# Attention and two feed-forward layers on one core: where the first feed-forward block's operand is made

## The chip, the cores and the metric

The kernel runs on one core of one Trainium2 chip. A core has a matmul engine (TensorE, PE in the rows), three engines for element-wise work (VectorE or DVE, ScalarE or ACT, GpSimd or POOL), a queue engine that here issues all transfers (SyncE, SP), 16 DMA engines, an on-chip memory (SBUF) and eight accumulator banks (PSUM) of 128 partitions by 512 floats. DRAM lies outside. The metric is the device time of one launch in microseconds; the time before is the median of three runs.

## The reference

Inputs are q, k, v of shape 4 x 8 x 576 x 64 (batches, heads, tokens, width), a memory per head, and the weights of two feed-forward layers (512 to 2048 to 512). Cut to what matters:

```python
a = softmax(q @ k.T / 8, causal); local = a @ v
mem = (phi(q) @ M_prev) / (phi(q) @ z_prev + 1e-6)        # phi(x) = elu(x) + 1
x = g * mem + (1 - g) * local                             # g = sigmoid(beta), per head
x = x as 2304 tokens x 512
x = (s * relu(x @ w_in)**2 + b) @ w_out                   # layer 1
h = x @ w_in2; x = (max(h, 0) + alpha * min(h, 0)) @ w_out2   # layer 2
```

All is float32 in and out.

## The kernel before, in words

**Precision.** The feed-forward matmuls work on the type fp32r, in which a float32 operand is given as two parts: a rounded one (h) and what the rounding left (l). A product is three matmuls: h by h, h by l, l by h. Weights and activations are split like this: a cast on ScalarE (or VectorE) writes h, a subtract on VectorE writes l.

**Attention.** Batches 0 to 3 are worked on in order, in each four pairs p of heads. A pair's 576 tokens are cut into two sets g (256 tokens, and 320 tokens with the last 64 in a chunk of their own). For each set TensorE makes scores, VectorE adds the mask and finds the extreme, ScalarE takes the exponential, the weights are scaled and turned, and TensorE accumulates the output of both heads (128 rows by 256 or 320 tokens) in a PSUM bank called `ok` (L697 to L722). In batch 0 any of the eight banks may be used, in later batches three. For batches 0 and 1 (`WHOLE`) the bank is copied as it is into an SBUF slot `xt` by ScalarE or VectorE, whichever is free first (L728 to L731). Once both sets are there, the pair's 576 tokens are stored into the DRAM tensor `x1` (L754).

**Feed-forward.** Layer 1 works on blocks of tokens: block 0 has 512 (of batch 0's 576), blocks 1 and 2 have 320, the others 288. Layer 2 has blocks of 512. `load_x` (L919 to L954) fetches a block's operand from `x1`: for block 0 these are four loads of 128 rows by 512 tokens (L934), each followed by a cast on ScalarE (L943) and a subtract on VectorE (L945) into the tile `xr`. A load waits for the stores that it reads. For each f of 16, g1 makes the hidden values (12 matmuls, L844 to L846, into one bank `hb`), Relu and Square on ScalarE (L858, L859) and a split (L866, L867) follow, and g2 accumulates the output in four banks (12 matmuls, L878 to L880).

**Weights.** Layer 1's weights come in 32 halves (16 f, w_in and w_out), as pairs of integers, and are put together and split: five operations each, four on VectorE and a cast on ScalarE (L790 to L804); the last, L802, completes the half. The load of f waits until pair min(3, f) of batch 0 is in `x1` (L786).

**Order.** Nothing runs by program order: every operation is entered with an engine, a duration, what it reads and writes, and a priority (`op`, L90), and a planner (`order`, L122) simulates the engines and writes a fixed list for each. An operation's default priority is its number, so attention comes in order; block splits have priority -3, the hidden values' -1, the block matmuls 10,000,000 and up, so that they fill the time that attention leaves on TensorE. Batch 0's slots may lie in memory that the last weights use later (`early`). A slot is taken and freed in the plan. The keys `("xh", s, d)` and `("xl", s, d)` stand for the operand's parts; block 0's g1 waits for those of s = 0 and 1 and all four d (L848 to L851), since its operand takes the room of two smaller blocks.

Of the kernel before, what the change touches and what calls it, by code (L numbers as in the profile page):

```python
# [6 lines left out]
F32 = mybir.dt.float32  # L7
# [5 lines left out]
ALU = mybir.AluOpType  # L13
AX = mybir.AxisListType

B, H, S, D = 4, 8, 576, 64
# [5 lines left out]
NBIG, NB = 512, 320  # L22
# [19 lines left out]
WHOLE = (0, 1)  # L42
# [29 lines left out]
class Plan:  # L72
# [17 lines left out]
    def op(self, eng, dur, fn, r=(), w=(), prio=None, bytes_=0, claim=()):  # L90
        i = len(self.ops)
        deps, late = set(), set()
        for k in r:
            if k in self.writer:
                deps.add(self.writer[k])
            self.readers.setdefault(k, []).append(i)
        for k in w:
            if k in self.writer:
                deps.add(self.writer[k])
            late.update(self.readers.get(k, ()))  # L100
            self.writer[k] = i
            self.readers[k] = []
        late -= deps
        late.discard(i)
        deps.discard(i)
        slots = []
        for k in list(r) + list(w):
            s = k[0] if isinstance(k, tuple) else k
            if isinstance(s, Slot) and s not in slots:
                slots.append(s)  # L110
                s.left += 1
        self.ops.append((eng, dur, fn, deps | late, i + self.lean if prio is None else prio, bytes_, slots, late, claim))
        return i
# [181 lines left out]
def t_dve(n, rate=1.04, extra=0.0):  # L295
    return 69 + n * rate + extra


def t_act(n, fixed=93.0, extra=0.0):
    return fixed + n * 0.834 + extra  # L300


def build(tc, kp, vd, qp, mzd, beta8, sb2, win1, wout1, win2, wout2, alpha, outT):
    nc = tc.nc
    win1, wout1, win2, wout2 = (w.bitcast(I32) for w in (win1, wout1, win2, wout2))
    V, A, T = nc.vector, nc.scalar, nc.tensor
    plan = Plan(NSLOT, 3 * XF)
    plan.edge = NSLOT - XS
    op = plan.op
    ATT, MOE, LATE = 0, 10 ** 7, 400  # L310

    with tc.tile_pool(name="sb", bufs=1) as sb, tc.tile_pool(
        name="ps", bufs=1, space=bass.MemoryType.PSUM
    ) as ps, tc.tile_pool(name="dr", bufs=1, space=bass.MemoryType.DRAM) as dr, tc.manual_schedule():
        x1 = dr.tile([128, NP, NT], F32, name="x1")
# [53 lines left out]
        def at(s, n, dt=F32):  # L369

            if s.place < NSLOT:
                t, j = (pool, s.place) if s.place < NSLOT - XS else (poolx, s.place - NSLOT + XS)
                v = t[:, j * GW:(j + s.size) * GW]
            else:
                f, j = divmod(s.place - NSLOT, 3)
                v = room[KF - XF + f][:, j * GW:(j + s.size) * GW]
            return (v if dt == F32 else v.bitcast(dt))[:, 0:n]
# [8 lines left out]
            out=mask[:, S - 128:], in_=mask[:, S - 128:], pattern=[[-1, 128]],  # L386
# [3 lines left out]
        for r in (0, 64):  # L390
            op("POOL", 150, lambda r=r: nc.gpsimd.tensor_copy(out=mask2[r:r + 64, S // 2 - 64:], in_=mask[r:r + 64, S - 128 + r:S - 64 + r]),
               r=["mask"], w=["mask2"])
# [7 lines left out]
        def consts2():  # L400
# [9 lines left out]
            out=ident, in_=ident, pattern=[[-1, 128]], compare_op=ALU.is_equal, fill=0.0, base=0, channel_multiplier=1),  # L410
           r=["ident"], w=["ident"])
# [8 lines left out]
        def bank_at(bk):  # L420
            return banks[bk.place - NSLOT - 3 * XF]
# [6 lines left out]
        def either(kind, a_dur, a_fn, d_dur, d_fn, **kw):  # L428

            ways = {"ACT": (a_dur, a_fn)}  # L430
            if kind in FLEX:
                ways["DVE"] = (d_dur, d_fn)
            plan.either(ways, **kw)
# [180 lines left out]
        def pair(b, p, sqp, sa, sv, xt):  # L614
# [4 lines left out]
               r=gate(b * H + 2 * p, KG, KG0), prio=-8 if b + p == 0 else None, w=[sk], bytes_=512 * S)  # L619
# [5 lines left out]
            for g, cs in enumerate(SETS):  # L625
                ch0 = cnt["ch"]
                o0 = AT[cs[0]]
# [97 lines left out]
                    return at(xt, S)[:, o0:o0 + qn]  # L725


                if b in WHOLE:  # L728
                    either("x", t_act(qn, 50), lambda xr=xr, qn=qn, ok=ok: A.copy(out=xr(), in_=bank_at(ok)[:, 0:qn]),
                           t_dve(qn), lambda xr=xr, qn=qn, ok=ok: V.tensor_copy(out=xr(), in_=bank_at(ok)[:, 0:qn]),  # L730
                           r=[ok], w=[(xt, g)])  # L731
                else:
                    un = vsc[:, j, 1:2]
                    either("x", t_act(qn, 50, 93), lambda xr=xr, qn=qn, ok=ok: A.activation(
                        out=xr(), in_=bank_at(ok)[:, 0:qn], func=AF.Copy, scale=un),
                        t_dve(qn, 1.04, 60), lambda xr=xr, qn=qn, ok=ok: V.tensor_scalar(
                        out=xr(), in0=bank_at(ok)[:, 0:qn], scalar1=un, scalar2=None, op0=ALU.mult),
                        r=[ok, ("un", j)], w=[(xt, g)])
# [3 lines left out]
        def attention(b):  # L742
            marks.append(len(plan.ops))
            memory(b)
            for p in range(NP):

                plan.lean = VLEAN
                sv = values(b, p)
                plan.lean = FLEAN
                sp_, sa = features(b, p)  # L750
                plan.lean = 0
                xt = Slot(RES["xt"], b == 0)
                pair(b, p, sp_, sa, sv, xt)
                op("SP", 475, lambda p=p, xt=xt: nc.sync.dma_start(out=x1[:, p, b * S:(b + 1) * S], in_=at(xt, S)),  # L754
                   r=[(xt, g) for g in range(2)], w=[("x1", b, p)], bytes_=512 * S)

# [54 lines left out]
        def x_of(n, xs, lo, d):  # L813

            if xs == 2:
                return cut(xr2(), n, KD * lo + d)
            if n == NBIG:
                return cut(xr_, n, KD * lo + d)
            return cut(xr_, n, 2 * KD * xs + KD * lo + d, NB)
# [99 lines left out]
        def load_x(layer, blk, t0, n, xs):  # L919
            step = GW // n  # L920
            for u in range(0, KD, step):
                s = Slot(RES["x"])
                if layer == 1:
                    src = x1[:, u:u + step, t0:t0 + n]
                    rk = [("x1", b, u + e) for e in range(step) for b in range(t0 // S, (t0 + n - 1) // S + 1)]
                else:
                    src = y1[:, u:u + step, t0:t0 + n]
                    rk = [("y1", j, u + e) for e in range(step) for j, (a, m) in enumerate(BLOCKS[1])
                          if a < t0 + n and t0 < a + m] + ["claimed"]

                def xr(s=s):
                    return at(s, step * n).rearrange("p (d n) -> p d n", d=step)

                op("SP", 475, lambda xr=xr, src=src: nc.sync.dma_start(out=xr(), in_=src), r=rk,  # L934
                   w=[s] + [("xset", x) for x in ((0, 1, 3) if xs == 3 else (xs,))], bytes_=512 * step * n,
                   prio=-2 if layer == 2 and blk > 0 else None)
                for e in range(step):
                    d = u + e
                    def X(lo, d=d):
                        return x_of(n, xs, lo, d)  # L940

                    if layer == 1:
                        op("ACT", t_act(n), lambda X=X, e=e, xr=xr: A.copy(out=X(0), in_=xr()[:, e, :]),  # L943
                           r=[s], w=[("xh", xs, d)], prio=-3)
                        op("DVE", t_dve(n), lambda X=X, e=e, xr=xr: V.tensor_tensor(  # L945
                            out=X(1), in0=xr()[:, e, :], in1=X(0).bitcast(F32), op=ALU.subtract),
                           r=[s, ("xh", xs, d)], w=[("xl", xs, d)], prio=-3)
                    else:
                        bc = bcs[:, d:d + 1]
                        op("ACT", t_act(n, 93, 180), lambda X=X, e=e, xr=xr, bc=bc: A.activation(  # L950
                            out=X(0), in_=xr()[:, e, :], func=AF.Identity, bias=bc), r=[s, ("bcs", d)], w=[("xh", xs, d)], prio=-3)
                        op("DVE", t_dve(n, 1.04, 60), lambda X=X, e=e, xr=xr, bc=bc: V.scalar_tensor_tensor(
                            out=X(1), in0=xr()[:, e, :], scalar=bc, in1=X(0).bitcast(F32), op0=ALU.add, op1=ALU.subtract),
                           r=[s, ("xh", xs, d), ("bcs", d)], w=[("xl", xs, d)], prio=-3)  # L954

        def moe(layer, blk, xs):
            t0, n = BLOCKS[layer][blk]
            load_x(layer, blk, t0, n, xs)
            for f in range(KF):
                if layer == 1 and blk == 0:  # L960
                    weights(win1, wout1, f, 1)
                if f == 0 and (layer, blk) == (1, 1):
                    flush()
                    op("ACT", 400, ones, r=["one", ("g2", KF - 1)],
                       w=["gr"] + [(x, j) for x in ("gt", "gh", "gl") for j in range(2)])

                if layer == 1 and n == NBIG and pend[0] is not None:
                    flush()
                gj = g1(layer, n, xs, f)
                if pend[0] is not None:  # L970
                    flush()
                pend[0] = (layer, blk, f, gj)
# [78 lines left out]
```

## Time and profile before

| what | value |
|---|---|
| median of three runs | 1017.6 us (1016.55 to 1017.99) |
| the profiled execution's own time | 1017.4 us |
| its span, first to last instruction | 1015.7 us |
| mean granted TensorE clock | 0.993 of 2.4 GHz |
| TensorE busy | 997.8 us (98%), 6648 matmuls |
| VectorE busy | 584.1 us (58%) |
| ScalarE busy | 461.3 us (45%) |

The busy time of an engine is the time in which at least one of its instructions runs. Matmuls overlap: each row's duration is longer than the step to the next. Digits in the page's slices are tenths; one of forty slices is 25.4 us. The clock is given as a part of 2.4 GHz, so that 0.50 is 1.2 GHz.

### The profile page before, as it was taken

How to read it: one execution, taken by the hardware profiler on the slowest of the kernel's cores; microseconds unless marked ns; L12 is line 12 of the kernel's file. 1: busy time of each engine (PE TensorE's matmuls, PEld its weight loads, DVE VectorE, ACT ScalarE, POOL GpSimd, SP SyncE). 2: the span in 40 equal slices, each digit the busy share in tenths (PEclk: the TensorE clock that was granted, in tenths of full speed). 3: DMA queues.
4: the chain of work that ended last, by engine and by line, in shares of the span. 5: the costliest groups of instructions: out<-in, count | busy, mean ns of one | idle time of the engine just before them, and what ended most of it. 6: DMA issues, size and time to landing. Idle time of an engine off the chain costs nothing.

```text
span 1015.7 us, 16933 instructions
## 1 busy us (share of the span) xinstructions
PE 997.8 (98%) x6648; PEld 846.0 (83%) x6648; DVE 584.1 (58%) x1389; ACT 461.3 (45%) x1113; POOL 5.1 (0%) x29
## 2 busy tenths in 40 slices
PE   7979999999999999999999999999999999999998
PEld 5757777778889888899999998888888888888898
DVE  7999987566555556543121779965434533443454
ACT  7866766677666677644444653222101111210111
POOL 1000000000000000000000000000000000000000
PEclk9979999999999999999999999999999999999999
DMA  4475433163564436542000555312000200100010
GB/s 146 164 257 174 159 137 128 49 143 90 113 147 115 71 82 150 104 140 88 1 24 2 169 169 166 116 62 83 1 1 1 73 1 1 42 1 1 1 43 21
DMA packets 85599, 87.12 MB, mean 86 GB/s; under 512 B 56336, under 2 KB 63504, under 8 KB 85520
## 3 DMA queue, kind: packets, MB, share of 16 engines
q1 hardware_dynamic: 85520, 86.05, 29.3%
q8 instruction: 52, 0.85, 0.3%
q14 instruction: 27, 0.22, 0.1%
HBM read 58.76 MB, written 14.16 MB: 72 GB/s over the span
## 4 chain that ended last, share of the span: by engine, by line
PE 95%; DVE 3%; ACT 1%; DMA 0%; issue 0%; SPq 0%; ACTq 0%; DVEq 0%
PE yb L878 14%; PE yb L880 13%; PE yb L879 13%; PE hb L844 9%; PE hb L845 8%; PE hb L846 8%; PE sp L846 3%; PE sp L845 3%; PE sp L844 3%; PE sp L716 2%; PE sp L663 2%; PE ob L845 2%; PE ob L844 2%; PE ob L846 2%; PE ob L663 1%; PE sp L551 1%
## 5 line engine op out<-in xcount | busy, mean ns | idle before, releaser
L878 PE MATMUL yb<-gr,wt 128*128 128x512 f32 (+4 forms) x768 | 264.6, 345 | 0.1
L880 PE MATMUL yb<-gr,wt 128*128 128x512 f32 (+4 forms) x768 | 259.6, 338 | 0.0
L879 PE MATMUL yb<-gr,wt 128*128 128x512 f32 (+4 forms) x768 | 259.4, 338 | 0.0
L844 PE MATMUL hb<-xr,wt 128*128 128x288 f32 (+3 forms) x528 | 176.4, 334 | 1.4 <-ACT gt L858 1.4
L845 PE MATMUL hb<-xr,wt 128*128 128x288 f32 (+3 forms) x528 | 170.5, 323 | 0.0
L846 PE MATMUL hb<-xr,wt 128*128 128x288 f32 (+3 forms) x528 | 170.2, 322 | 0.0
L878 PEld LDWEIGHTS yb<-gr,wt 128*128 128x128 f32 x768 | 144.4, 188 | 23.8 <-issue 8.1
L867 DVE TENSOR_TENSOR gr<-gt,gr 128x288 fp32r<-128x288 f32 (+3 forms) x152 | 81.5, 536 | 140.0 <-ACT gr L866 139.4
L880 PEld LDWEIGHTS yb<-gr,wt 128*128 128x128 f32 x768 | 144.5, 188 | 14.7 <-DVE gr L867 0.2
L879 PEld LDWEIGHTS yb<-gr,wt 128*128 128x128 f32 x768 | 144.6, 188 | 13.4
L866 ACT CAST gr<-gt 128x288 fp32r<-128x288 f32 (+3 forms) x152 | 75.3, 495 | 144.8 <-DVE gt L864 136.1
L844 PEld LDWEIGHTS hb<-xr,wt 128*128 128x128 f32 x528 | 99.5, 188 | 17.2 <-issue 8.9
L846 PEld LDWEIGHTS hb<-xr,wt 128*128 128x128 f32 x528 | 99.6, 189 | 5.8
L858 ACT ACTIVATE gt<-hb 128x288 f32<-128x288 f32 (+2 forms) x112 | 49.8, 444 | 118.7 <-PE hb L846 118.0
L845 PEld LDWEIGHTS hb<-xr,wt 128*128 128x128 f32 x528 | 99.6, 189 | 4.3
L866 ACT CAST gr<-mz 128x512 fp32r<-128x512 f32 (+1 forms) x40 | 23.1, 578 | 158.0 <-DVE mz L864 157.9
L846 PE MATMUL sp<-xr,wt 128*128 128x512 f32 (+1 forms) x160 | 59.4, 371 | 0.0
L845 PE MATMUL sp<-xr,wt 128*128 128x512 f32 (+1 forms) x160 | 59.3, 371 | 0.0
L844 PE MATMUL sp<-xr,wt 128*128 128x512 f32 (+1 forms) x160 | 59.2, 370 | 0.0
L648 DVE CUSTOM_DVE_ANT_0 sp<-sp,mask 128x384 f32<-128x384 f32 (+4 forms) x81 | 40.8, 514 | 25.4 <-PE sp L663 14.8
L859 ACT ACTIVATE gt<-gt 128x288 f32<-128x288 f32 (+2 forms) x112 | 53.5, 478 | 2.4
L867 DVE TENSOR_TENSOR gr<-mz,gr 128x512 fp32r<-128x512 f32 (+1 forms) x40 | 25.6, 639 | 25.3 <-ACT gr L866 25.3
(352 smaller groups left out, 1452.7 us busy)
## 6 DMA issues: line engine op xcount, KB each, us to landing
pool<-wout SPq DMA_DIRECT2D x20, 512.0 KB, 4.5
pool<-win SPq DMA_DIRECT2D x19, 512.0 KB, 3.7
room<-wout SPq DMA_DIRECT2D x12, 512.0 KB, 4.1
room<-win SPq DMA_DIRECT2D x11, 512.0 KB, 3.8
pool<-y SPq DMA_DIRECT2D x18, 256.0 KB, 3.3
out_t<-pool SPq DMA_DIRECT2D x16, 256.0 KB, 2.1
x<-poolx SPq DMA_DIRECT2D x10, 288.0 KB, 2.5
pool<-qp SPq DMA_DIRECT2D x9, 288.0 KB, 4.2
```

The source lines that it names most:

```text
L648: op("DVE", t_dve(kn, 1.04, 60 if before is not None else 0), lambda: V.tensor_tensor_reduce(out=bank_at(bk)[:, 0:kn], in0=bank_at(bk)[:, ...
L663: T.matmul(bank_at(bks[odd])[:, 0:nk], half(sqp, odd, AT[c], 128), half(sk, odd, 0, nk), start=True, stop=True)
L844: T.matmul(H_, W_h, X_h, start=(d == 0), stop=False)
L845: T.matmul(H_, W_h, X_l, start=False, stop=False)
L846: T.matmul(H_, W_l, X_h, start=False, stop=(d == KD - 1))
L858: op("ACT", t_act(n, 50), lambda: A.activation(out=t_, in_=H_, func=AF.Relu), r=[hk, "gr"], w=[tk], prio=-1)
L859: op("ACT", t_act(n), lambda: A.activation(out=t_, in_=t_, func=AF.Square), w=[tk], prio=-1)
L866: op("ACT", t_act(n), lambda: A.copy(out=G_h, in_=t_), r=[tk], w=[("gh", gj)], prio=-1)
L867: op("DVE", t_dve(n), lambda: V.tensor_tensor(out=G_l, in0=t_, in1=G_h.bitcast(F32), op=ALU.subtract), r=[tk, ("gh", gj)], w=[("gl", gj)], ...
L878: T.matmul(Y, W_h, G_h, start=(f == 0), stop=False)
L879: T.matmul(Y, W_l, G_h, start=False, stop=False)
L880: T.matmul(Y, W_h, G_l, start=False, stop=(f == KF - 1))
```

## The change

For batch 0 the output bank `ok` is no longer copied as a whole. Of each set, the tokens that belong to block 0 (256 of the first set, 256 of the second) are cast from PSUM into the h part of `xr` by ScalarE, and VectorE subtracts that from PSUM into the l part. The 64 tokens left of the second set are copied to the slot `xt` by either engine and stored into `x1`; the store has 64 tokens in place of 576. `load_x` is not called for block 0 of layer 1. The two splits of a pair use the keys s = g = 0 and 1, and have the default priority in place of -3. All else is as it was, and the planner makes the whole order anew.

```diff
-                if b in WHOLE:
+                if b == 0:
+                    m = min(qn, NBIG - o0)
+
+                    def X(lo, o0=o0, m=m):
+                        return x_of(NBIG, 0, lo, p)[:, o0:o0 + m]
+
+                    op("ACT", t_act(m, 50), lambda X=X, m=m, ok=ok: A.copy(out=X(0), in_=bank_at(ok)[:, 0:m]),
+                       r=[ok], w=[("xh", g, p)])
+                    op("DVE", t_dve(m), lambda X=X, m=m, ok=ok: V.tensor_tensor(
+                        out=X(1), in0=bank_at(ok)[:, 0:m], in1=X(0).bitcast(F32), op=ALU.subtract),
+                       r=[ok, ("xh", g, p)], w=[("xl", g, p)])
+                    if m < qn:
+                        either("x", t_act(qn - m, 50), lambda m=m, qn=qn, ok=ok: A.copy(out=at(xt, qn - m), in_=bank_at(ok)[:, m:qn]),
+                               t_dve(qn - m), lambda m=m, qn=qn, ok=ok: V.tensor_copy(out=at(xt, qn - m), in_=bank_at(ok)[:, m:qn]),
+                               r=[ok], w=[(xt, g)])
+                elif b in WHOLE:
...
-                op("SP", 475, lambda p=p, xt=xt: nc.sync.dma_start(out=x1[:, p, b * S:(b + 1) * S], in_=at(xt, S)),
-                   r=[(xt, g) for g in range(2)], w=[("x1", b, p)], bytes_=512 * S)
+                t0 = NBIG if b == 0 else 0
+                op("SP", 475, lambda p=p, xt=xt, t0=t0: nc.sync.dma_start(out=x1[:, p, b * S + t0:(b + 1) * S], in_=at(xt, S - t0)),
+                   r=[(xt, g) for g in range(2)], w=[("x1", b, p)], bytes_=512 * (S - t0))
...
-            load_x(layer, blk, t0, n, xs)
+            if (layer, blk) != (1, 0):
+                load_x(layer, blk, t0, n, xs)
```

## Rows read from the trace of the kernel before

**Rows 1.** The page, the span in 40 slices: TensorE's busy tenths and its clock.

```profile
PE   7979999999999999999999999999999999999998
PEclk9979999999999999999999999999999999999999
```

**Rows 2.** Busy time by stretch: stretch, length, engines (instructions), clock, DMA share, GB/s.

```profile
64.70:78.00 13.30, 9.14 (x32) 7.07 (x32) 13.08 (x40) 8.98 (x24) 0.00 (x0) 0.62 0.80 279
78.00:85.00 7.00, 6.31 (x43) 3.33 (x43) 6.99 (x18) 3.92 (x11) 0.00 (x0) 1.00 0.61 181
85.00:456.00 371.00, 371.00 (x2994) 308.57 (x2994) 239.90 (x683) 251.44 (x640) 2.02 (x11) 1.00 0.46 120
```

**Rows 3.** The same view, of two gaps and two stretches at the lower clock.

```profile
54.20:56.40 2.20, 0.10 (x3) 0.04 (x2) 2.20 (x8) 1.38 (x6) 0.00 (x0) 1.00 0.87 225
57.75:60.90 3.15, 3.01 (x15) 2.61 (x14) 2.44 (x6) 2.17 (x4) 0.00 (x0) 0.50 0.86 316
64.78:66.49 1.71, 0.00 (x1) 0.01 (x1) 1.71 (x6) 1.71 (x5) 0.00 (x0) 1.00 0.89 240
67.87:77.98 10.11, 8.13 (x29) 6.75 (x30) 10.11 (x32) 5.87 (x17) 0.00 (x0) 0.50 0.77 280
```

**Rows 4.** Timeline, 63 to 75 us: start, duration, engine, line, instruction [idle before <-releaser].

```profile
63.55 0.43 ACT L729 COPY room<-hb 128x320 f32<-128x320 f32 x1 [1.84 <-PE hb L716]
64.01 0.33 SPq L754 DMA_DIRECT2D x<-room  x1
66.14 0.33 SPq L934 DMA_DIRECT2D pool<-x  x1
...
66.49 0.91 PE L663 MATMUL sp<-pool 64*128 64x384 f32 x2 [1.71 <-ACT poolx L641]
...
71.99 0.60 ACT L943 CAST xr<-pool 128x512 fp32r<-128x512 f32 x1
73.09 0.69 DVE L945 TENSOR_TENSOR xr<-pool,xr 128x512 fp32r<-128x512 f32 x1
74.55 0.78 PE L844 MATMUL hb<-xr,wt 128*128 128x512 f32 x1
```

**Rows 5.** Timeline: weight halves completed (L802), and a later g1 group's first matmul.

```profile
42.74 0.65 DVE L802 TENSOR_TENSOR wt<-pool,wt 128x512 fp32r<-128x512 f32 x1
62.09 0.65 DVE L802 TENSOR_TENSOR wt<-room,wt 128x512 fp32r<-128x512 f32 x1
65.99 0.68 DVE L802 TENSOR_TENSOR wt<-room,wt 128x512 fp32r<-128x512 f32 x1
94.08 0.68 DVE L802 TENSOR_TENSOR wt<-room,wt 128x512 fp32r<-128x512 f32 x1
127.39 0.48 PE L844 MATMUL hb<-xr,wt 128*128 128x512 f32 x1
```

**Rows 6.** By line: duration ns min/median/max, first and last start; then one timeline row.

```profile
L729 ACT COPY poolx<-yb x1: 372/372/372, 30.6 to 30.6; 128x256 f32<-128x256 f32 x1
L516 DVE TENSOR_TENSOR pool<-ob,nrm x2: 398/406/415, 60.1 to 71.0; 128x256 f32<-128x256 f32 x2
L730 DVE COPY room<-sp x1: 415/415/415, 17.7 to 17.7; 128x256 f32<-128x256 f32 x1
57.39 0.29 DVE L561 COPY poolx<-yb 128x128 f32<-128x128 f32 x1
```

**Rows 7.** Timeline of TensorE: a g1 group's start and the next g2 group's.

```profile
84.71 0.50 PE L844 MATMUL hb<-xr,wt 128*128 128x512 f32 x1 [0.69 <-ACT gt L858]
87.61 0.40 PE L878 MATMUL yb<-gr,wt 128*128 128x512 f32 x1
```

**Rows 8.** Timeline of ScalarE: batch 1's last output, block 1's first cast.

```profile
192.11 0.43 ACT L729 COPY pool<-sp 128x320 f32<-128x320 f32 x1 [0.55 <-PE sp L716]
216.92 0.81 ACT L943 CAST xr<-pool 128x320 fp32r<-128x320 f32 x2
```

**Rows 9.** Busy time by stretch: attention with block 0, and block matmuls alone.

```profile
85.00:222.00 137.00, 137.00 (x877) 102.61 (x877) 107.27 (x286) 94.16 (x228) 0.59 (x4) 1.00 0.40 125
660.00:860.00 200.00, 200.00 (x863) 161.67 (x862) 91.14 (x133) 31.75 (x52) 0.00 (x0) 1.00 0.09 28
```

## The prediction

> **What bounds the kernel now.** I read the page's slices first, then the stretches by stage, then the timeline around the one stage that is not full, and the durations of single instructions last.
>
> TensorE sets the time. In the page's forty slices its row stands at 9 almost everywhere; apart from the first and the last slice, the one gap is the slice from 51 to 76 us, where TensorE's busy share and its clock both read 7 [rows 1]. By stage: from 85 to 456 us TensorE is busy 371.00 of 371.00 us at clock 1.00; from 64.7 to 78 us it is busy 9.14 of 13.30 us at a mean clock of 0.62, while VectorE is busy 13.08 [rows 2]. The finer stretches show the two faults of that stage: no matmul at all between 64.78 and 66.49, and the clock at 0.50 (1.2 GHz instead of 2.4) from 67.87 to 77.98, in which TensorE is busy 8.13 us [rows 3].
>
> What ends that stage is the first block's operand. The timeline shows the chain [rows 4]: the last output of batch 0 is copied out of PSUM by ScalarE at 63.55 (0.43 us), its store is issued at 64.01, the load back at 66.14, the cast runs at 71.99, the subtract from 73.09 to 73.78, and the first matmul of block 0 starts at 74.55. So 9.8 us pass between the end of the copy (63.98) and the end of the split (73.78). In that time TensorE has only batch 1's attention to do, and waits for it (1.71 us before L663 for ScalarE [rows 4]).
>
> The block's weights are not what it waits for. Each weight half is complete after its L802. Four of these run between 42.74 and 62.74, the first and the last of them and the fifth, which ends at 66.67, stand in [rows 5]. So f = 0 and f = 1 are there, both halves, before the last output is out.
>
> **The change, part by part.**
>
> *The operand comes earlier.* After the last output, ScalarE casts 256 columns out of PSUM, VectorE subtracts 256 columns. The nearest rows are a ScalarE copy of 256 PSUM columns, 0.37 us, and a VectorE operation on 256 PSUM columns, 0.41 [rows 6]. VectorE can have one weight operation of 0.68 in front. The end of the split is then between 64.4 (63.55 + 0.37 + 0.1 + 0.41) and 65.1, instead of 73.78. TensorE stops at 64.78 in the trace, so the block's matmuls can start about where the gap began.
>
> Is there enough to do? Block 0's pass over one f is two groups of twelve matmuls, g1 and g2; one group takes 2.9 us at full clock (a g1 group starts at 84.71, the g2 group behind it at 87.61 [rows 7]). f = 0 and 1 hold four groups, 11.6 us. The stage's present work would take 9.14 − 8.13 / 2 = 5.07 us at full clock [rows 2, 3], so 13.30 − 5.07 = 8.2 us more are wanted, and they are there before f = 2 is complete at all (the little that block 0 does from 74.55 on is in the 5.07).
>
> What goes is the same 8.2 us, in two parts: the idle time, 13.30 − 9.14 = 4.16 us [rows 2], and the lost half of 8.13 us at 1.2 GHz, 4.07 us [rows 3]. The clock fell after gaps (2.10 of 2.20 us without a matmul in 54.2 to 56.4, then 0.50 from 57.75 [rows 3]; 1.71 us at 64.78, then 0.50 from 67.87); with block 0 in the gaps from 64.8 on, nothing of that kind is left before the second fall.
>
> What is late next: the hidden-layer bank. g1 of the next f waits until the Relu has emptied the only bank: 0.69 us at 84.71 [rows 7], the whole idle time of 78 to 85 [rows 2]. At that rate (0.69 in 7 us) the 13.3 us would keep 1.3 us; since the row's own 0.69 falls away when the start moves ahead, I charge 0.6 net (bounds 0 and 1.3).
>
> *More work on VectorE inside batch 0.* Eight subtracts of 256 columns from PSUM at 0.41 are 3.3 us. Before, batch 0 had three subtracts of 512 at 0.69 (the fourth came at 73.09) and one output copy of 0.41 (L730 [rows 6]): 2.5 us. So VectorE gets 0.8 us more, and up to 1.1 more if all four copies of the 64 columns fall to it (0.29 at most, the row of a 128-column copy [rows 6]). ScalarE does eight casts of 0.37 (3.0) in place of seven copies of about 0.40 (0.37 and 0.43 for the two sizes [rows 4, 6]) and three casts of 0.60 [rows 4] (4.6 together): 1.6 less. TensorE's banks stay occupied for the cast and the subtract instead of one copy. Bounds for batch 0's end: 1.6 us earlier (all of it ScalarE's relief) and 1.9 later (all of it VectorE's work). I take 0.9 later, near VectorE's own 0.8, because VectorE has hardly an idle moment in the neighbouring stretch (13.08 of 13.30 [rows 2]). The weights' VectorE work, which the planner ranks lower, can slip instead; that is the cover, and it would make this term nothing.
>
> *The transfers.* Four loads of 256 KB and nine tenths of four stores of 288 KB go, with the four SP issues (0.33 us for the one at 66.14 [rows 4]) and the wait of SP for the store to land in front of the last of them. No data of block 0 are late by the smaller stores; the next block's 64 tokens are not read before batch 1 is finished at 192 us [rows 8]. The weights of f = 0 to 3 remain gated by those stores; each is issued after one more small copy, at most 0.3 us later. I cost this at nothing: the gated weights are far ahead (the thirteenth half, f = 6, starts its last step at 94.08 and its matmuls at 127.39 [rows 5]). If the cover were gone it would be 0.3 us; the freed DMA time (some 2 MB) can only help, by how much is in the second rival.
>
> *Does the gain last to the end?* Work done by 78 us is work not to do later, if TensorE stays fed. Two places could end that. Weights: the margin above is 33 us. Block 1's operand: it may be written only when block 0's first products are over; batch 1's last output is out at 192.11, the cast for block 1 runs at 216.92 [rows 8], so block 0 can end over 20 us earlier before block 1 is late. Both margins hold 8 us.
>
> One more reading is possible. TensorE's row of 371.00 in 371.00 [rows 2] says that nothing is free behind 85 us. The weight loads say something else: they are busy 102.61 of 137.00 us (75%) from 85 to 222, but 161.67 of 200.00 (81%) from 660 to 860, where nothing but block matmuls runs back to back [rows 9]. If 81% is full, the first of these stretches has 137 x (1 - 75 / 81) = 10 us of room, enough to swallow 6.7. I take the busy row, because the attention's matmuls, of other shapes, can account for the lower share as well; the other reading is the third rival. The Trainium skill, "Perfetto Trace Analysis", section "Identifying the Most-Contended Engine", prefers that other reading: matmul busy time, it says, is a poor measure of how near TensorE is to its limit, and the busy share of the weight loads a better one. By it the sum would be about nothing, by the busy row it is -6.7; the trace shows both shares and no run so far tells which counts.
>
> *Sum.* −8.2 + 0.6 + 0.9 = −6.7 us against the profiled execution's 1017.4 us (its span of 1015.7 and 1.7 us around it): 1010.7. That execution lies 0.2 us under the median of the runs, 1017.6, so no correction is made.
>
> **The rivals.**
>
> *The clock stays low (1014.7).* TensorE works through one list in a fixed order. If an attention matmul that waits for ScalarE stands ahead of block 0's in that list, the gaps shrink but some remain and the clock falls as before. Then the 4.07 us are not won: −4.16 + 0.6 + 0.9 = −2.7. For it: 1.71 us at L663. Against it: from 78 to 85, with block 0 in the list, only 0.69 us is idle. Chance 0.14.
>
> *More than the stage (1007.1).* With fewer transfers, buffers and long VectorE operations the earlier fault may go too: 2.10 us without a matmul at 54.2 and half of 3.01 us at 1.2 GHz [rows 3], 3.6 us together. For it: a cast and a subtract for block 0 and weight operations lie in that stretch. Against it: the block's operand cannot be there yet, so only luck in the order does it. Chance 0.13.
>
> *Given back later (1017.4).* TensorE is not the limit behind 85 us: attention sets the pace there, block 0's matmuls of after 74.55 had room in it, and taking some of them away early only leaves that room larger. The 10 us by the weight loads [rows 9] hold all 6.7. Partial forms lie between. For it: VectorE's 107.27 of 137.00 [rows 9]. Against it: no idle time of TensorE in 371 us. Chance 0.12.
>
> *Batch 0 grows by more (1020.0, slower).* Each of eight outputs now holds its PSUM bank for a cast, a hand-over and a subtract, and VectorE, which is nearly full, is behind it. If the whole delay lands on the chain: 0.37 + 0.41 and a wait like the 0.50 us between the cast's end (72.59) and the subtract's start (73.09) [rows 4], 1.28 us each, 10.2 us in all; −8.2 + 0.6 + 10.2 = +2.6. It decides from 0.95 us per output on (7.6 / 8). Against it: batch 0 rotates eight banks, and weight work can step back. Chance 0.09.
>
> **How the numbers follow.** My forecast has 0.52. Its own range is 1007.6 (−8.2 − 1.6) to 1012.4 (−8.2 + 1.3 + 1.9), from the bounds of the charges. 0.2% (2 us) is about what a measurement of this kernel can tell from no change. Faster: forecast, first and second rival, 0.79. Same: third rival, 0.12. Slower: 0.09. The range of 1005.5 to 1016.0 holds the forecast (nearly all of it), the first two rivals and partial forms of the third, 8 in 10.
>
> **What would show it.** Right: the first L844 at about 65 us, two L945-like subtracts of 256 columns per pair and no load of the first block; the stretch from 65 to 78 full at clock 1.00; the fall at 57.75 still there. The gain should be all in hand by 85 us. Wrong: batch 0's last L716 later than 65 us (fourth rival), a second fall of the clock with block 0 running (first), idle time or late weights behind 85 us (third).

## The result and the profile after

The changed kernel takes 1005.6 us (median of four runs, 1005.18 to 1007.41) against 1017.45 before (four runs, three of which gave the 1017.6 stated before the change): a ratio of 0.9888, 95% interval 0.9871 to 0.9905, or 11.8 us less. The forecast was 1010.7, range 1005.5 to 1016.0: right in sign and place, too small by 5.1 us, and the measured time lies only 0.1 us inside the range's lower end.

The profiled execution's span fell from 1015.7 to 1003.5 us, by 12.2. The first lines of the two pages split this in two: TensorE's busy time went from 997.8 to 992.3 (5.5 less, for the same 6648 matmuls, so more of them ran at the higher clock), and its idle time from 17.9 to 11.2 (6.7 less). The page of the kernel after:

```profile
span 1003.5 us, 16924 instructions
PE 992.3 (99%) x6648; PEld 841.5 (84%) x6648; DVE 583.7 (58%) x1395; ACT 457.9 (46%) x1111; POOL 5.2 (1%) x29
PE   7999999999999999999999999999999999999998
PEclk9999999999999999999999999999999999999999
```

The third slice, 7 in both lines of [rows 1], is now 9. The stretches, first two of the kernel before that were not shown, then the kernel after (columns as in [rows 2]):

```profile
0.00:50.00 50.00, 43.61 (x398) 31.08 (x398) 42.18 (x164) 40.45 (x118) 3.05 (x18) 1.00 0.46 157
50.00:64.70 14.70, 12.41 (x119) 9.72 (x114) 13.99 (x41) 9.99 (x26) 0.00 (x0) 0.88 0.59 191
```

```profile
0.00:50.00 50.00, 43.99 (x378) 31.05 (x380) 41.11 (x162) 41.08 (x124) 2.96 (x17) 1.00 0.40 136
50.00:64.70 14.70, 13.26 (x148) 10.07 (x145) 14.57 (x48) 10.00 (x29) 0.15 (x1) 1.00 0.50 160
64.70:78.00 13.30, 13.21 (x81) 8.41 (x80) 13.29 (x43) 10.08 (x25) 0.00 (x0) 1.00 0.61 211
78.00:85.00 7.00, 7.00 (x37) 5.73 (x36) 6.46 (x17) 4.58 (x13) 0.00 (x0) 1.00 0.55 170
85.00:456.00 371.00, 371.00 (x3027) 311.12 (x3026) 244.66 (x694) 252.81 (x642) 2.09 (x11) 1.00 0.48 124
```

Read against [rows 2, 3], the 12.2 us between these two profiles come to this:

| stretch | what went | us |
|---|---|---|
| 64.7 to 78 | idle 4.16 to 0.09; half of 8.13 us at 1.2 GHz | 4.07 + 4.07 |
| 78 to 85 | idle 0.69 to 0 | 0.69 |
| 50 to 64.7 | idle 2.29 to 1.44; half of 3.01 us at 1.2 GHz | 0.85 + 1.50 |
| 0 to 50 | idle 6.39 to 6.01 | 0.38 |
| behind 456 | idle 4.30 to 3.67; a wait of 0.68 at 458.29 is gone | 0.63 |

Together 12.2. In the timeline of the kernel after, around batch 0's last output (chosen rows, which answer to [rows 4]):

```profile
60.68 1.89 PE L716 MATMUL yb<-room,pool 128*64 128x128 f32 x40
62.62 0.37 ACT L735 CAST xr<-yb 128x256 fp32r<-128x256 f32 x1 [1.28 <-PE yb L716]
62.89 0.22 ACT L741 COPY room<-yb 128x64 f32<-128x64 f32 x1
63.13 0.33 SPq L771 DMA_DIRECT2D x<-room  x1
63.85 0.42 DVE L737 TENSOR_TENSOR xr<-yb,xr 128x256 fp32r<-128x256 f32 x1
63.86 0.48 PE L861 MATMUL hb<-xr,wt 128*128 128x512 f32 x1
```

The cast runs at 62.62, the subtract from 63.85 to 64.27, and the first block matmul starts at 63.86, 10.7 us before the 74.55 of [rows 4]. It does not even wait for the subtract: it reads the part of pair 0, and the last pair's part is needed nine matmuls later. All eight casts and subtracts by line, with the small copies (ns, first and last start):

```profile
L735 ACT CAST xr<-yb x6: 363/372/373, 25.8 to 62.6; 128x256 fp32r<-128x256 f32 x6
L735 ACT CAST xr<-sp x2: 369/376/384, 17.2 to 43.0; 128x256 fp32r<-128x256 f32 x2
L737 DVE TENSOR_TENSOR xr<-yb,xr x6: 414/416/420, 26.4 to 63.8; 128x256 fp32r<-128x256 f32 x6
L737 DVE TENSOR_TENSOR xr<-sp,xr x2: 414/416/417, 17.8 to 43.4; 128x256 fp32r<-128x256 f32 x2
L741 ACT COPY room<-yb x1: 218/218/218, 62.9 to 62.9; 128x64 f32<-128x64 f32 x1
L742 DVE COPY room<-yb x3: 214/223/223, 26.2 to 50.9; 128x64 f32<-128x64 f32 x3
```

The bounds from [rows 4, 6] for these durations were good: 0.37, 0.42 and 0.22 us. The split as a whole took longer than reckoned, 1.70 us from the end of the last product (62.57) to the end of the subtract, where the prediction has 0.9 to 1.6: the subtract stood behind two other operations of VectorE. For the reason just given this cost nothing.

### The profile page after: what moved, and what is told of

It reads as the page before. It is cut to its first block, busy times and chain, and to the rows that moved or that the text cites. A ratio compares the mean times of both kernels' runs of the same rounds, so it can differ in the third digit from the quotient of the medians.

```text
span 1003.5 us, 16924 instructions
## 1 busy us (share of the span) xinstructions
PE 992.3 (99%) x6648; PEld 841.5 (84%) x6648; DVE 583.7 (58%) x1395; ACT 457.9 (46%) x1111; POOL 5.2 (1%) x29
## 4 chain that ended last, share of the span: by engine, by line
PE 95%; DVE 3%; ACT 1%; issue 0%; DMA 0%; SPq 0%; ACTq 0%; DVEq 0%
PE yb L895 14%; PE yb L897 13%; PE yb L896 13%; PE hb L861 9%; PE hb L862 8%; PE hb L863 8%; PE sp L863 3%; PE sp L862 3%; PE sp L861 3%; PE sp L663 2%; PE sp L716 2%; PE ob L861 2%; PE ob L862 2%; PE ob L863 2%; PE ob L716 2%; PE ob L663 1%
## 5 line engine op out<-in xcount | busy, mean ns | idle before, releaser
L861 PE MATMUL hb<-xr,wt 128*128 128x288 f32 (+3 forms) x528 | 176.0, 333 | 0.0
L861 PEld LDWEIGHTS hb<-xr,wt 128*128 128x128 f32 x528 | 99.2, 188 | 16.6 <-issue 9.4
L861 PE MATMUL sp<-xr,wt 128*128 128x512 f32 (+1 forms) x160 | 59.3, 370 | 0.0
L648 DVE CUSTOM_DVE_ANT_0 sp<-sp,mask 128x512 f32<-128x512 f32 (+4 forms) x83 | 41.2, 509 | 20.9 <-PE sp L663 11.7
```

What stands on the lines that cost most here:

```text
L648: op("DVE", t_dve(kn, 1.04, 60 if before is not None else 0), lambda: V.tensor_tensor_reduce(out=bank_at(bk)[:, 0:kn], in0=bank_at(bk)[:, ...
L861: T.matmul(H_, W_h, X_h, start=(d == 0), stop=False)
```

## The experiments

The theory: the operand of the last pair was what the first block waited for; its trip through DRAM cost the stage from 65 to 78 us, 8.9 us with the 0.7 behind it. (Not all of the 9.8 us of that trip are transfers. In the kernel before, the store landed 2.1 us after its issue and the load 4.4 us, so the data were there at 70.5; the cast began 1.5 us later and the subtract 0.5 us after the cast's end [rows 4], some 2 us of waiting in the lists of ScalarE and VectorE.) Rivals: the transfers and copies taken away are the gain; or the new order is, whatever made it new.

**Which pair counts.** In `last_pair` only p = 3 is split from PSUM, in `first_pairs` only p = 0 to 2:

```diff
-                if b == 0:
+                if b == 0 and p in DIRECT:
...
-                t0 = NBIG if b == 0 else 0
+                t0 = NBIG if b == 0 and p in DIRECT else 0
...
             for u in range(0, KD, step):
+                if (layer, t0) == (1, 0) and u in DIRECT:
+                    continue
```

> Only the last pair of batch 0 (p = 3) makes its part of the operand from PSUM; pairs 0 to 2 go through DRAM as before. Theory (the block waits for the last pair's trip alone): the stage from 65 to 78 us is full at clock 1.00, which is worth 8.2 us, and 0.7 of the idle time behind it; 1008.5, between 1006 and 1011 with what the new order does to batch 0. Rival (the gain is the transfers and copies taken away): a quarter of it stays, 1014.5. Rival (the gain is the new order of batch 0, whatever made it new): anything, with no tie to the first block matmul's start.

> The reverse: pairs 0 to 2 from PSUM, only the last pair through DRAM. Theory: the first block matmul starts at 73 to 75 us as before, the stage stays half empty, 1017.5 within 3 for the new order. Rival (transfers and copies): three quarters of the gain, 1008.7.

Measured: `last_pair` 1009.1 us, ratio 0.9918 (0.9894 to 0.9942); `first_pairs` 1018.5, ratio 1.0007 (0.9995 to 1.0019). One pair of four brings most of the gain, the other three by themselves none. The first block matmul of `last_pair`; then the operand's last subtract in `first_pairs` and its first block matmul:

```profile
60.86 0.50 PE L862 MATMUL hb<-xr,wt 128*128 128x512 f32 x1
```

```profile
74.44 0.69 DVE L965 TENSOR_TENSOR xr<-pool,xr 128x512 fp32r<-128x512 f32 x1
75.57 0.50 PE L862 MATMUL hb<-xr,wt 128*128 128x512 f32 x1
```

The last pair's trip is the cause, and the rival that three quarters of the transfers are three quarters of the gain has fallen. Two things blur the picture. In `first_pairs` the stage was fuller than in [rows 2], with batch 1's attention, and the time was lost again later, by a wait at the first matmul of block 1 and a fall of the clock behind it (0.57 as the mean of 225 to 229 us):

```profile
64.70:78.00 13.30, 11.18 (x60) 6.98 (x60) 11.90 (x37) 8.35 (x22) 0.00 (x0) 0.74 0.70 220
```

```profile
223.49 0.41 PE L862 MATMUL hb<-xr,wt 128*128 128x320 f32 x1 [3.24 <-ACT gt L876]
```

And the 3.5 us by which `last_pair` is slower than the changed kernel need not be the other pairs' transfers: its profile has a wait of 2.02 us at 214.65 that the changed kernel's has not, and a mean clock of 0.87 from 64.7 to 78.

**What the copies, loads and stores are worth.** Four kernels keep parts of the old way beside the new one, with no use made of them. `traffic_kept` copies and stores the whole output and loads block 0 as before:

```diff
-                    if m < qn:
-                        either("x", t_act(qn - m, 50), ...
+                    either("x", t_act(qn, 50), lambda xr=xr, qn=qn, ok=ok: A.copy(out=xr(), in_=bank_at(ok)[:, 0:qn]), ...
...
-                t0 = NBIG if b == 0 else 0
+                t0 = 0
...
-            if (layer, blk) != (1, 0):
-                load_x(layer, blk, t0, n, xs)
+            load_x(layer, blk, t0, n, xs)
...
-                for e in range(step):
+                for e in range(0 if (layer, t0) == (1, 0) else step):
```

In `traffic_kept` block 0's matmuls do not wait for these loads (an edit to the load's list of writes, not shown). `copies_kept` has the first of these edits only, and stores the last 64 columns of the full copy; `stores_kept` has the first two; `loads_kept` is the changed kernel with four loads of 256 KB:

```diff
+            else:
+                for u in range(KD):
+                    s = Slot(RES["x"])
+                    op("SP", 475, lambda s=s, u=u: nc.sync.dma_start(out=at(s, n), in_=kp[0, u][:, 0:n]),
+                       r=[("x1", 0, u)], w=[s], bytes_=512 * n)
```

> All four pairs from PSUM, but the whole output is still copied and stored (576 tokens) and block 0's four loads of 256 KB are still made, into slots that nobody reads. Theory: the stage stays full, 1006 to 1009; what it loses against 1005.6 is the price of the extra copies (eight of 0.4 us) and transfers. Rival (the transfers were what delayed the work): back to 1014 or more.

> The changed kernel, with the whole output of batch 0 still copied to a slot (eight copies of 256 or 320 columns beside the splits), but only the 64 tokens stored and no load of the first block. It parts what the run traffic_kept mixed (1014.4, batch 0's last output product begun at 66.6 in place of 60.7 us). Theory now: batch 0's end is set by ScalarE and VectorE, so the copies alone bring most of those 6 us back: 1010 to 1014. Rival (the transfers delay batch 0, through the memory's load for batch 1 and the weights): 1006 to 1008.

> The changed kernel, with four loads of 256 KB that nobody reads at the places of block 0's four (from the keys' array, since the output is no longer in DRAM). Theory: transfers alone cost little, 1005.5 to 1008. Rival: the transfers are most of what traffic_kept lost, 1010 to 1014.

> As copies_kept (1008.7), and the whole 576 tokens of each pair of batch 0 are stored, but block 0 is not loaded. It stands between copies_kept and traffic_kept (1014.4), whose 5.7 us are open. If the stores themselves are the cause: 1012 to 1015. If it is the loads behind them, which wait on SP for the stores and go ahead of batch 1's loads, or the order that comes out with them: 1008 to 1010.

| kernel | us | ratio to before, interval | last product of batch 0 begins | first block matmul |
|---|---|---|---|---|
| changed | 1005.6 | 0.9888 (0.9871 to 0.9905) | 60.68 | 63.86 |
| loads_kept | 1006.0 | 0.9888 (0.9872 to 0.9905) | 60.73 | 63.90 |
| copies_kept | 1008.7 | 0.9914 (0.9900 to 0.9929) | 61.84 | 65.37 |
| traffic_kept | 1014.4 | 0.9966 (0.9954 to 0.9978) | 66.56 | 69.74 |
| stores_kept | 1016.7 | 0.9996 (0.9986 to 1.0005) | 66.59 | 69.97 |

My expectation of 1006 to 1009 for `traffic_kept` failed, and its rival, 1014 or more, was met. The loads cost nothing that shows (0.4 us). With the copies the kernel is 3.1 us slower, and TensorE is idle 8.8 us of the first 50, against 6.0 in the changed one. That this is the price of the copies is not shown: another order of the changed kernel alone is 3.3 us slower, with 7.3 us idle there (p190, below). For `copies_kept` I had said 1010 to 1014, or 1006 to 1008 by the rival; it lies between. The rest came with the full stores. `stores_kept`, for which I had 1012 to 1015 or 1008 to 1010, is slower than either, as slow as the kernel before though its operand never leaves the chip. Its timeline of SP and TensorE shows how:

```profile
54.86 0.33 SPq L770 DMA_DIRECT2D x<-room  x1
55.24 0.42 SPq L447 DMA_DIRECT2D poolx<-vd  x1
55.72 0.44 SPq L437 DMA_DIRECT2D mz<-mzd  x1
...
59.11 0.69 PE L506 MATMUL sp<-mz,pool 128*128 128x130 f32 x4 [2.13 <-DMA mz<-mzd]
61.17 0.48 PE L551 MATMUL yb<-ident,pool 128*128 128x128 f32 x1 [1.38 <-ACT pool L536]
...
66.59 2.09 PE L716 MATMUL hb<-pool 128*64 128x128 f32 x40
```

Batch 1's memory is loaded behind the third pair's store (the code ties it to that store, L437). Here it goes out behind a store of 288 KB and a load of 320 KB, and TensorE, whose list has batch 1's L506 ahead of batch 0's last work, waits 2.13 us for it and 1.38 us for ScalarE after that. Its clock falls (0.50 from 60.4 to 67.0), and batch 0's last product begins at the end of that fall, 5.9 us later than in the changed kernel:

```profile
50.00:64.70 14.70, 11.18 (x109) 9.10 (x108) 13.99 (x41) 10.76 (x31) 0.00 (x0) 0.85 0.55 171
64.70:78.00 13.30, 12.64 (x94) 9.42 (x94) 10.23 (x34) 8.72 (x25) 0.15 (x1) 0.91 0.51 180
```

In `copies_kept` the same load is issued at 55.98, with only a store of 32 KB in front, and no wait for it appears. That points to the size of the store, but `last_pair` speaks against it. There the memory's load stands behind just such a store and such a load:

```profile
50.22 0.33 SPq L772 DMA_DIRECT2D x<-room  x1
50.63 0.38 SPq L448 DMA_DIRECT2D poolx<-vd  x1
51.07 0.45 SPq L438 DMA_DIRECT2D mz<-mzd  x1
54.34 0.71 PE L507 MATMUL ob<-mz,pool 128*128 128x130 f32 x4 [0.62 <-DMA mz<-mzd]
59.04 1.89 PE L717 MATMUL yb<-poolx,pool 128*64 128x128 f32 x40
```

The three are issued 4.6 us earlier than in `stores_kept`, TensorE waits 0.62 us, and batch 0's last product begins at 59.04, earlier than in the changed kernel. So a full store in front of that load does not by itself cost the gain; in `stores_kept` it comes with an order that issues it late, and what made that order so late is not shown. `traffic_kept`, with more transfers, is 2.3 us faster than `stores_kept`: there too the order has its part.

**What the clock alone is worth.** `fill` is the kernel before with 24 more matmuls, entered behind batch 0's last output:

```diff
+                    if f == 0:
+                        for i in range(24):
+                            op("PE", t_r(NBIG), lambda: T.matmul(ybank[3][:, :NBIG], wt(0, 0, 0)[:, 0:128], x_of(NBIG, 0, 0, 0), start=True, stop=True),
+                               r=[("wi", "h", 0), ("xh", 0, 0), ("last",)], w=[("fill", i)], prio=MOE - 1)
```

> The kernel before, with 24 extra matmuls of 512 columns (their result is overwritten) behind batch 0's last output, so that TensorE has something to run while the operand travels; the operand comes as late as before. Asks what the clock alone is worth. If the lost half of 8.1 us counted by itself, 4.1 us would come back: 1013.4. Theory: attention in that stage is not held up by TensorE, so only the matmuls between 74.5 and 78 us gain, 3.4 us at half speed: 1.7 us, 1015.8. If the clock falls all the same: 1017.5.

Measured 1013.7 us, ratio 0.9964 (0.9954 to 0.9975): 3.3 us less, by medians, with some 5.6 us of useless work more (24 steps of 0.23 us). I had said 1.7 us; the first case of the expectation, 1013.4, was nearer. The rows of `fill`, the stage and then the last store's issue and the operand's cast, subtract and first matmul:

```profile
64.70:78.00 13.30, 12.37 (x80) 8.31 (x78) 12.72 (x40) 7.98 (x23) 0.00 (x0) 1.00 0.74 257
```

```profile
62.88 0.33 SPq L754 DMA_DIRECT2D x<-room  x1
71.13 0.60 ACT L943 CAST xr<-pool 128x512 fp32r<-128x512 f32 x1
72.74 0.68 DVE L945 TENSOR_TENSOR xr<-pool,xr 128x512 fp32r<-128x512 f32 x1
73.06 0.48 PE L844 MATMUL hb<-xr,wt 128*128 128x512 f32 x1
```

The clock stays at 1.00. The cast comes 0.86 us earlier than in [rows 4] and the first block matmul 1.5, but slow matmuls that hold up the split are not the reason: the store was issued 1.1 us earlier, in an execution whose clock had not fallen at 57.75 (see the last experiment), and from the store to the cast it is 8.25 us here and 7.98 there. What is shorter is the time from the subtract's start to the first block matmul, 0.32 us against 1.46; whether the clock or the new order did that is not shown. So some 3 of the stage's 8.2 us come back when TensorE is kept busy, in the order that the planner then made; why it is more than 1.7 stays open. The rest came only with the operand.

**How much is the order's luck.** Each kernel twice more, with one number of the planner changed that only makes another order:

```diff
-    SAME = {"PE": 0.0, "DVE": 130.0, "ACT": 145.0}
+    SAME = {"PE": 0.0, "DVE": 120.0, "ACT": 145.0}
```

(d120), or `SYNC = {"PE": 190.0}` in place of 200 (p190).

> The kernel before, with one number of the planner changed (VectorE's hand-over 120 in place of 130 ns), which does nothing but write another order from the first microseconds on. Theory (2.9 us of the 11.8 are the luck of the order in batch 0): the stage around 70 us keeps its gap, the total scatters by 3 us or so, 1014.5 to 1020.5. Rival (the order is worth less than 0.5 us): 1017 to 1018.

> As the run before_d120 with another number (TensorE's hand-over 190 in place of 200 ns). Theory: 1014.5 to 1020.5 and the gap before the first block matmul stays. Rival: 1017 to 1018.

> The changed kernel with VectorE's hand-over 120 in place of 130 ns in the planner, another order. Theory: the stage from 65 to 78 us stays full, and what goes beyond 8.9 us comes and goes with the order of batch 0: 1004 to 1011. Rival (all 11.8 us belong to the change): 1005 to 1006.5.

> The changed kernel with TensorE's hand-over 190 in place of 200 ns in the planner. Theory: 1004 to 1011, the stage from 65 to 78 us full. Rival: 1005 to 1006.5.

| order | before | after |
|---|---|---|
| as given | 1017.5 | 1005.6 |
| d120 | 1017.5, ratio 1.0008 (0.9999 to 1.0017) | 1006.8, ratio 0.9903 (0.9888 to 0.9918) |
| p190 | 1018.0, ratio 1.0005 (0.9991 to 1.0018) | 1008.9, ratio 0.9926 (0.9909 to 0.9942) |

(All ratios are to the kernel before in its given order.) Before, the order hardly moves the median: the theory's scatter of 3 us is not there. It is there between executions of one order: the ten of p190 go from 1015.62 us, at a mean clock of 0.997, to 1019.53 at 0.993. After, the orders scatter by 3.3 us, as expected, and the given order is the best of three. The means are 1017.7 and 1007.1: the change is worth 10.6 us over these orders (10.0 by the ratios), and 1.5 of the 11.8 us are the luck of one. The rival that the order is the gain has fallen too: none of the three orders of the kernel before comes near.

**The first fall of the clock.** The kernel before once more:

> The kernel before once more, one look. In its first profile the clock fell to 0.50 at 57.75 us after a gap of 2.1 us; in the run fill, with the same instructions up to 62 us and the same gap, it did not fall there. If that fall comes and goes between executions, this look may be without it, and 1.5 us of the difference between the two first profiles are not the change's. If it belongs to the order, it is there again.

It took 1016.7 us. Its rows, the gap (a little later than in [rows 3]) and the stretch in which the clock stood at 0.50 there; then the same two of `fill`, whose TensorE list is that of the kernel before up to 62 us; and last, batch 0's last product in [rows 4]'s execution, in `before_again` and in `fill`:

```profile
54.70:57.00 2.30, 0.20 (x4) 0.18 (x3) 2.30 (x8) 1.48 (x5) 0.00 (x0) 1.00 0.69 223
57.75:60.90 3.15, 2.53 (x22) 2.13 (x20) 3.15 (x10) 2.42 (x6) 0.00 (x0) 1.00 0.95 355
```

```profile
54.20:56.40 2.20, 0.13 (x1) 0.13 (x2) 2.19 (x8) 1.38 (x5) 0.00 (x0) 1.00 0.80 221
57.75:60.90 3.15, 2.53 (x25) 2.06 (x25) 3.15 (x9) 2.53 (x5) 0.00 (x0) 1.00 0.83 296
```

```profile
61.62 1.89 PE L716 MATMUL hb<-poolx,pool 128*64 128x128 f32 x40
61.03 1.89 PE L716 MATMUL hb<-poolx,pool 128*64 128x128 f32 x40
60.49 1.89 PE L716 MATMUL hb<-poolx,pool 128*64 128x128 f32 x40
```

The same gap, and no fall, twice: the fall does not belong to the order. Without it there is a wait of 0.62 us at 59.7 or 59.2 in its place, batch 0 ends 0.6 to 1.1 us earlier, and `before_again` took 0.7 us less than the execution with the fall. It is not rare, though. For 60 more executions of the kernel before, the record has the mean clock: 38 stand at 0.993 or less, like the profile with the fall (0.993), and 22 at 0.994 or 0.995, like `before_again` (0.995). As far as the mean clock tells them apart, the fall is the more common case, and the time does not show it: the medians are 1017.0 and 1017.1 us. So the 1.5 us of that fall in the table of the result describe one pair of profiles; as a part of the 11.8 us they are not shown.

## Why the prediction was right, and where it was too small

**The place and the mechanism held.** The operand's trip through DRAM was what left TensorE half empty. The first block matmul (L844, now L861) was forecast at about 65 us and came at 63.86; the stage was to give 8.2 us and gave 8.14 (4.07 and 4.07). `last_pair` and `first_pairs` show that it is the last pair's trip. The forecast's own range, 1007.6 to 1012.4, was missed by 2.0 us; it was the rivals' room in the whole range that held the result. One sign failed: the fall at 57.75 was to be still there, and the clock stood at 1.00.

**The charge of 0.6 us for the hidden bank was wrong.** Nothing of it was left (0.09 us idle), and the 0.69 of 78 to 85 went as well. In the given order attention lies between the groups and covers the Relu. Against the sum: 1.3 us.

**The term of 0.9 us for batch 0 was not met, and why is open.** Batch 0's last product ended at 62.57, not at 63.51. I had looked at VectorE's 0.8 us more and not at ScalarE's 1.6 less (1.4 as it came: L735 and L741 together are 3.2 us, against the 4.6 reckoned for before), and that would fit. But without the first fall of the clock the kernel before ended batch 0 at 62.92 (`before_again`) and 62.38 (`fill`); the two other orders of the changed kernel end it at 63.77 and 62.70, and `last_pair`, which keeps the copies of three pairs, at 60.93. The clock and the order move this end by more than the term, so that its sign is not shown. My bound of 1.6 us earlier held the 0.9. Against the sum: 0.9 charged and not lost, and 1.2 us of idle time that went before 64.7, together 2.1 us. With 1.5 us at the lower clock before 64.7 and 0.6 behind 456, of which the sum had nothing, this makes up the difference between -6.7 and -12.2.

**The second rival was nearer in number (1007.1) and is only in part borne out in cause.** It named the gap at 54.2 and the fall behind it. In the profile after there is no fall, and the longest wait there is 1.43 us in place of 2.10. No run ties either to the operand. The fall comes and goes without any change, and 1.5 us of the 11.8 is the luck of the order. The prediction put both down to luck, and nothing here says otherwise.

**The third rival fell.** The gain was in hand at 85 us, and no idle time came back: TensorE is busy 371.00 of 371.00 us behind it, and the time fell by the whole. From 85 to 222 us the weight loads are busy 104.45 of 137.00 us (76%), against 75% in [rows 9], so the lower share there was not room. By the reading that the Trainium skill prefers ("Perfetto Trace Analysis", "Identifying the Most-Contended Engine") the gain would have been swallowed; in this case the trace sides with the busy row. A gain can be given back behind 85 us all the same, by waits: `first_pairs` and `last_pair` lost 3.24 and 2.02 us in waits for ScalarE near the start of block 1, and p190 of the changed kernel is idle 1.07 us behind 85.

**The fourth rival did not decide here.** Its cause, banks held for a cast and a subtract, shows in no run. That batch 0 can grow enough to take the gain is shown by `stores_kept`, where it ended at 68.7 us and the whole gain was gone, by another way: the late load of batch 1's memory. The point from which growth decides was reckoned at 7.6 us in all; there it took 6.1 us of batch 0, a fall of the clock and a wait of 1.95 us at 218.39. I had costed the freed stores at nothing. In the given order they may be worth something; `last_pair`, which keeps three of the four and ends batch 0 early, shows that full stores need not cost anything.

**The first rival did not occur.** In the profiles of all three orders of the changed kernel the clock stood at 1.00 from 50 to 85 us.

## What to carry to other kernels

When a filler of low priority becomes ready only through one last transfer, its start is what to look at: three of four parts made earlier were worth nothing by themselves here, the last one most of the gain. Count idle time and the time at the lower clock as two terms of the same gap; keeping the clock up with useless work gave back some 3 of the 8.2 us by itself. Before a part of a difference between two profiles is given a cause, take a second profile of the same kernel. And where a planner writes the order, time a few orders of either kernel before a microsecond or two is ascribed to a change.

## What was not expected of the hardware

After a gap of 2.1 us without a matmul in the same list of instructions, the granted clock stood at 0.50 from 57.75 to 60.90 us in one execution and at 1.00 in two others. After the later and more broken gap from 64.8 us on it fell in both profiles of the kernel before: 0.62 as the mean of 64.7 to 78 in both.
